# Linear attention and channel mix on one core: first two batches transposed on TensorE, v loads on the software queue, engine orders planned anew

## The chip, the cores and the metric

The kernel runs on one core of a Trainium2 chip (trn2). The metric is the device time of one execution in microseconds (us). TensorE is called PE here, VectorE DVE, ScalarE ACT, GpSimd POOL and SyncE SP, as in the profile.

## What is computed

Eight batches, eight heads, 576 positions, head width 64, 128 features. The attention output of a batch, [576, 512], is the input of a channel mix with hidden width 1024.

```python
def phi(x):
    proj = np.einsum('bhsd,df->bhsf', x, w_phi)
    proj = proj - np.max(np.abs(proj), axis=-1, keepdims=True)
    return np.concatenate([np.exp(proj), np.exp(-proj)], axis=-1)
q_p, k_p = (phi(q), phi(k))
kv = np.einsum('bhsf,bhsd->bhfd', k_p, v)
z = np.sum(k_p, axis=2)
num = np.einsum('bhsf,bhfd->bhsd', q_p, kv)
den = np.einsum('bhsf,bhf->bhs', q_p, z)[..., None] + 1e-06
# num / den, as x [B, S, 512], goes into:
xk = mu_k * x + (1.0 - mu_k) * x_prev
xr = mu_r * x + (1.0 - mu_r) * x_prev
k = np.maximum(xk @ w_k, 0.0)
v = k * k @ w_v
r = 1.0 / (1.0 + np.exp(-(xr @ w_r)))
return (r * v).astype(np.float32)
```

## The kernel before

The unit of the attention part is a pair of heads; there are 32 pairs, four to a batch. A position is split as 64 rows times 9 columns, so that two heads fill the 128 partitions and a pair's k or q is a [128, 576] tile. The steps of a pair have short names in the code, which the texts use. PE projects q and k (`qp`, `kp`, L418); DVE takes the largest absolute value of each row and column group, negated (`rq` L435, `rk` L430); POOL writes it as two bf16 parts (`mh`, L454 and L455); PE transposes that (`mt`, L459), DVE copies it out of PSUM (`mc`, L463), and PE adds it to the projections of k and q (`ka` L468, `qt` L476 and L482). ACT takes the exponentials, two for k (`ea`, `eb`, L445) and two for q (`qa`, `qb`, L489). POOL copies v into a tile with a column of ones (`vc`, L439), PE forms kv (`kv`, L504 and L510), ACT evicts it (`kc`, L515), PE forms numerator and denominator (`nd`, L523 and L528), DVE divides (`rd`, L535 and L537), PE transposes the result (`xt`, L545), and DVE writes it to `xs` (`xe`, L551 to L556), takes the difference of neighbours (`df`, L560) and mixes (`xa`, `xb`, L566). The ninth column of k and of q is done for several pairs at once, in steps whose names end in `e` (`tp`, `rt`, `mhe` L342 and L343, `mte`, and so on).

When all four pairs of a batch are mixed, its channel mix follows in 512-column pieces: eight `h` (four matmuls each, L636), ACT's relu (`rl`, L643), POOL's square (`sq`, L650), four `r` with a tanh, and four `v` (eight matmuls each, L671), which DVE scales into `ob` (L678) and SP stores (L685). The last 128 columns of two batches are done together (L712 to L788).

Loads: for each batch POOL's software queue loads k and q (`lk`, `lq`, L256, f32 in HBM and bf16 in `nat`), SP transposes both with one DMA (`tr`, L265) into `qkT`, and SP loads v in f32 (`lv`, L261). Batch 0 is loaded in three parts: pair 0, pair 1, and pairs 2 and 3. There are two buffers each of `nat`, `qkT` and `vt`: the load of k of batch b can start when the transpose of batch b - 2 has read `nat`. The three weights are loaded on POOL's queue (L291).

The order of the work is not written out by hand. Each step is entered with `op(name, engine, width, due, fn, deps, alloc, rel)`, and `Plan.order` (L45) simulates the engines with these widths and the delays `LAG` and `SWITCH`: for each engine it looks at up to twelve steps whose dependences are done, takes those that can start within 0.12 of the earliest, and of these the one with the least `due`. The instructions of an engine are then emitted in that order, and each engine works through its own strictly in order. Due times come from a spacing of T = 8.2 per pair.

```python
op(f"lk{tag}", "POOL", 0.7, due, ld(0), alloc=al("nat"), chain="lk")
op(f"tr{tag}", "SP", 0.6, due, tr, [f"lk{tag}.d", f"lq{tag}.d"], alloc=al("qkT"),
   rel=[("nat", b)])
```

In the simulation `nat` counts as free when the SP step `tr` ends, and that is 0.6 wide; on the chip it is free when the transpose has landed.

Of the kernel before, what the change touches and what calls it, by code (L numbers as in the profile page):

```python
# [15 lines left out]
LAG = {"PE": 0.25, "ACT": 0.2, "DVE": 0.15, "POOL": 0.2, "SP": 0.05, "DMA": 1.8}  # L16


SWITCH = 0.12


class Plan:
# [4 lines left out]
    def __init__(self):  # L27
        self.ops = []
        self.by_name = {}
        self.last = {}  # L30

    def op(self, name, eng, w, due, fn, deps=(), alloc=(), rel=(), chain=None, mode=0):
# [6 lines left out]
        o = dict(name=name, eng=eng, w=w, due=due, fn=fn, deps=tuple(deps),  # L39
# [5 lines left out]
    def order(self, bufs, loose=()):  # L45
# [3 lines left out]
        self.mode = 0  # L49
        slots = {t: [None] * bufs[t] for t in loose}  # L50
# [15 lines left out]
        while len(out) < n:  # L66
            best = None
            for e, ql in queues.items():
# [44 lines left out]
            free[e] = t + o["w"]  # L113
            end[o["name"]] = free[e]
# [23 lines left out]
def kernel(  # L138
# [108 lines left out]
    def add_load(b, a0, a1, due, first):  # L247
# [20 lines left out]
        g = 1.0 * n  # L268
        op(f"lk{tag}", "POOL", 0.7, due, ld(0), alloc=al("nat"), chain="lk")
        op(f"lk{tag}.d", "DMA", g, due, None, [f"lk{tag}"])  # L270
        op(f"lq{tag}", "POOL", 0.7, due, ld(1), [f"lk{tag}"])
        op(f"lq{tag}.d", "DMA", g, due, None, [f"lq{tag}"])
        op(f"tr{tag}", "SP", 0.6, due, tr, [f"lk{tag}.d", f"lq{tag}.d"], alloc=al("qkT"),
           rel=[("nat", b)])
        op(f"tr{tag}.d", "DMA", 1.5 * n, due, None, [f"tr{tag}"])
        op(f"lv{tag}", "SP", 0.6, due + 0.1, ldv, alloc=al("vt"), chain="lv")
        op(f"lv{tag}.d", "DMA", g, due + 0.1, None, [f"lv{tag}"])

    parts = {b: [(0, NP)] for b in range(B)}
    parts[0] = [(0, 1), (1, 2), (2, 4)]  # L280
    for b in range(B):
        for i, (a0, a1) in enumerate(parts[b]):
            add_load(b, a0, a1, ((4 * b - 6) * T if b > 1 else -50 + 10 * b + i), i == 0)

    def part_of(b, a):
        for (a0, a1) in parts[b]:
            if a0 <= a < a1:
                return f"{b}.{a0}"
# [15 lines left out]
    op("wvs", "DVE", 1.2, 3.2 * T,  # L304
# [5 lines left out]
    def ptile(key, name):  # L310
        return psum.tile([128, 2, 512], FP, name=name, tag=f"P{plan.place[key]}")

    def motile(key, name):
        return psum.tile([128, 512], FP, name=name, tag=f"M{plan.place[key]}")

    def add_edge(b, a0, a1, first, due):
# [57 lines left out]
        def eqe():  # L374
# [29 lines left out]
    def add_pair(n):  # L404
# [3 lines left out]
        d0 = n * T  # L408
        pt = part_of(b, a)
# [163 lines left out]
        op("qp" + N, "PE", 0.25, d0, qp, [f"tr{pt}.d", "dve1"], alloc=[("P", ("P", "q" + N))], chain="qp",  # L573
# [257 lines left out]
```

## Time and profile before

| | |
|---|---|
| median of 2 runs | 414.72 us (414.13 to 415.3) |
| profiled execution | 413.09 us |
| its span, first to last instruction | 411.3 us |
| time around the span | 1.8 us |
| mean granted TensorE clock | 0.942 of full speed |
| HBM read, written | 33.62 MB, 9.44 MB |

The profile is one execution. The page gives each engine's busy time. The timeline lists instructions in order of time, with the idle time of the engine before them in brackets and what ended it. The view by windows gives busy time of each engine, granted clock and DMA share for stretches of 5 us. The waits list who waited for whom. DMA issues are listed with the time from issue to landing.

### The profile page before, as it was taken

The page shows a single profiled execution, that of the slowest core. Times are in us where ns is not written, and L with a number is a line of the kernel's source. Part 1 is how long each engine was busy: PE and PEld are TensorE (multiplying, and loading weights), DVE is VectorE, ACT ScalarE, POOL GpSimd, SP SyncE. Part 2 cuts the span into 40 slices and gives each one's busy share as a digit, 9 for nine tenths or more (in the row PEclk, how much of TensorE's full clock was granted, in tenths as well). Part 3 has the DMA queues.
Part 4 walks back from the last instruction along what each step waited for, and adds up shares of the span by engine and source line. Part 5 has one row for each costly group of instructions (what it writes and reads, how often), then busy time and mean ns, then how long its engine had stood idle before and what let it go on. Part 6 is the DMA issues. An engine that isn't in the chain of part 4 may idle for free. (4 is left out here: it accounts for less than half of the span.)

```text
span 411.3 us, 8965 instructions
## 1 busy us (share of the span) xinstructions
PE 307.0 (75%) x3712; PEld 169.8 (41%) x3758; DVE 254.1 (62%) x456; ACT 209.6 (51%) x309; POOL 137.5 (33%) x237
## 2 busy tenths in 40 slices
PE   0046347867859779977778679977896979979895
PEld 0025235532435445534425345534453534535352
DVE  2035437996749786694845886595859566666312
ACT  0035235725717846657327646659285555665340
POOL 6042241164341461553323163145013420341450
PEclk9999999596989999997969899999999689999999
DMA  8989999953595008921792007402720002202214
GB/s 203 241 138 240 176 201 227 129 92 115 108 178 165 2 2 153 226 97 27 134 241 50 2 2 142 105 0 39 129 55 0 2 15 56 62 0 45 61 26 102
DMA packets 59063, 41.01 MB, mean 100 GB/s; under 512 B 39952, under 2 KB 49808, under 8 KB 59024
## 3 DMA queue, kind: packets, MB, share of 16 engines
q1 hardware_dynamic: 48416, 28.39, 31.2%
q0 software_dynamic: 10608, 12.06, 18.6%
q8 instruction: 29, 0.48, 0.5%
q14 instruction: 10, 0.08, 0.1%
HBM read 33.62 MB, written 9.44 MB: 105 GB/s over the span
## 5 line engine op out<-in xcount | busy, mean ns | idle before, releaser
L650 POOL TENSOR_TENSOR kk<-krelu 128x512 bf16<-128x512 bf16 x64 | 67.1, 1062 | 98.9 <-ACT krelu L643 98.8
L445 ACT ACTIVATE k<-ps_k 128x1024 bf16<-128x1024 f32 x64 | 62.3, 1029 | 47.5 <-PE ps_k L468 33.5
L636 PE MATMUL ps_h<-xk,wk_bf 128*128 128x512 bf16 x233 | 66.9, 402 | 5.3 <-ACT krelu L643 1.7
L671 PE MATMUL ps_v<-wv_bf,kk 128*128 128x512 bf16 x245 | 62.7, 396 | 3.3 <-DVE ob L678 1.4
L489 ACT ACTIVATE q<-ps_qT 128x1024 bf16<-128x1024 f32 x64 | 62.3, 1036 | 5.3 <-PE ps_qT L482 5.2
L643 ACT ACTIVATE krelu<-ps_h 128x512 bf16<-128x512 f32 x64 | 38.3, 613 | 45.6 <-PE ps_h L636 40.0
L678 DVE SCALAR_TENSOR_TENSOR ob<-rt,ps_v 128x512 f32<-128x512 bf16 x32 | 22.0, 687 | 46.0 <-issue 21.0
L435 DVE TENSOR_REDUCE nm<-ps_q 128x8 f32<-128x1024 f32 x32 | 39.0, 1220 | 13.3 <-PE ps_q L418 13.2
L664 ACT ACTIVATE rt<-ps_r 128x512 bf16<-128x512 f32 x32 | 19.2, 601 | 50.7 <-PE ps_r L657 50.2
L430 DVE TENSOR_REDUCE nm<-ps_k 128x8 f32<-128x1024 f32 x32 | 39.0, 1218 | 4.6 <-PE ps_k L418 4.5
L657 PE MATMUL ps_r<-wr_bf,xr 128*128 128x512 bf16 x117 | 34.5, 401 | 5.1 <-ACT krelu L733 2.1
L671 PEld LDWEIGHTS <-kk 128*128 128x128 bf16 x256 | 24.1, 100 | 33.0 <-issue 8.2
L636 PEld LDWEIGHTS <-wk_bf 128*128 128x128 bf16 x256 | 22.8, 101 | 30.5 <-issue 9.3
L566 DVE SCALAR_TENSOR_TENSOR xr<-diff,mu_r_t,xs 128x576 bf16<-128x576 bf16 x32 | 33.5, 1046 | 0.0
L454 POOL CAST mhl<-nm 128x16 bf16<-128x16 f32 x32 | 6.8, 212 | 69.7 <-DVE nm L430 69.7
L566 DVE SCALAR_TENSOR_TENSOR xk<-diff,mu_k_t,xs 128x576 bf16<-128x576 bf16 x32 | 28.9, 903 | 1.1
L537 DVE TENSOR_TENSOR x_sc<-ps_nd,rden 128x640 bf16<-128x640 f32 x32 | 26.4, 824 | 1.1
L504 PE MATMUL ps_kv<-v,k 64*128 64x65 bf16 x1024 | 25.4, 202 | 2.0 <-ACT k L445 1.7
L504 PEld LDWEIGHTS <-k 64*128 64x128 bf16 x1024 | 22.6, 102 | 9.6 <-issue 6.8
L333 DVE TENSOR_REDUCE me<-ps_e 128x8 f32<-128x1024 f32 (+2 forms) x10 | 10.1, 1007 | 25.8 <-PE ps_e L327 25.8
L418 PEld LDWEIGHTS <-qkT 64*128 64x128 bf16 x512 | 18.5, 102 | 17.9 <-issue 14.4
L459 PE MATMUL ps_m<-ident,mhl 128*128 128x128 bf16 x32 | 7.6, 238 | 24.0 <-POOL mhl L455 21.7
(74 smaller groups left out, 451.2 us busy)
## 6 DMA issues: line engine op xcount, KB each, us to landing
out_dram<-ob SPq DMA_DIRECT2D x72, 128.0 KB, 2.4
vt<-in_v_dram SPq DMA_DIRECT2D x7, 1152.0 KB, 9.6
nat<-in_k_dram POOLq DMA_DIRECT2D x7, 576.0 KB, 6.7
nat<-in_q_dram POOLq DMA_DIRECT2D x7, 576.0 KB, 10.7
wk_bf<-in_moe_w_k_dram POOLq DMA_DIRECT2D x1, 1024.0 KB, 15.0
wv_bf<-in_moe_w_v_dram POOLq DMA_DIRECT2D x1, 1024.0 KB, 21.0
vt<-in_v_dram SPq DMA_DIRECT2D x2, 288.0 KB, 4.8
vt<-in_v_dram SPq DMA_DIRECT2D x1, 576.0 KB, 7.0
```

The source lines that it names most:

```text
L430: nc.vector.tensor_reduce(s["nm"][:, 0, :], s["k"].rearrange("p a (g f) -> p (a g) f", f=128), axis=AX.X, op=ALU.max, apply_absolute_value ...
L435: nc.vector.tensor_reduce(s["nm"][:, 1, :], s["q"].rearrange("p a (g f) -> p (a g) f", f=128), axis=AX.X, op=ALU.max, apply_absolute_value ...
L445: nc.scalar.activation(s[f"k{pn}"], s["k"].rearrange("p a (g f) -> p (a g) f", f=128), AF.Exp, scale=(1.0 if pn == 0 else -1.0))
L489: nc.scalar.activation(t.rearrange("f h (c p) -> f c h p", c=8), s["qT"].rearrange("f a (g h p) -> f (a g) h p", g=4, h=2), AF.Exp, scale= ...
L504: nc.tensor.matmul(ps[:, hh, pn * 65:(pn + 1) * 65], lhsT=s[f"k{pn}"][r, c, :], rhs=vb[r, a, 2 * g + par, :], start=(pn == 0 and c == 0), ...
L537: nc.vector.tensor_tensor(s["x"].rearrange("p (b s) d -> p b s d", b=2), ndv[:, :, :, 0:64], s["rd"].to_broadcast([128, 2, 5, 64]), op=ALU ...
L566: nc.vector.scalar_tensor_tensor(out=t[:, a, (b % 2) * S:(b % 2 + 1) * S], in0=s["d"], scalar=mu[:, a:a + 1], in1=xs[:, a, 0:S], op0=ALU.m ...
L636: nc.tensor.matmul(ps, lhsT=wk_bf[:, c, fc * 128:(fc + 1) * 128], rhs=xkt[bp][:, c, m0:m0 + 512], start=(c == 0), stop=(c == NDC - 1))
L643: nc.scalar.activation(s["kr", fc], s[fc], AF.Relu)
L650: nc.gpsimd.tensor_tensor(s["kk"][:, fc, :], s["kr", fc], s["kr", fc], op=ALU.mult)
L657: nc.tensor.matmul(ps, lhsT=xrt[bp][:, c, m0 + ci * 128:m0 + (ci + 1) * 128], rhs=wr_bf[:, c, :], start=(c == 0), stop=(c == NDC - 1))
L671: nc.tensor.matmul(ps, lhsT=s["kk"][:, fc, ci * 128:(ci + 1) * 128], rhs=wv_bf[:, fc, :], start=(fc == 0), stop=(fc == NFC - 1))
```

## The change

- **Batch 0, pair 0.** k is loaded in f32 by SP's hardware queue (`hk`) and q by ACT's (`hq`); DVE casts k into `nat` (`lk0.0.d`), ACT casts q (`lq0.0.d`).
- **Batches 0 and 1.** No DMA transpose. For each of the eight pairs PE transposes nine 128x128 blocks into one of the three double PSUM banks "P" (`pt`); DVE copies five of them to `qkT` (`pa`), ACT four (`pb`). Batch 1 is loaded in two parts.
- **v** of every batch is loaded on POOL's software queue, cast to bf16 on the way.
- **Order of POOL's queue.** `lk`, `lq`, `lv` of all batches stand in one chain: batches 0 and 1, the weights (before: behind the transpose of batch 1), then batches 2 to 7.
- **Plan.** Due times are now pair number times 8.90 plus an offset for each kind of step (table `OFF`). The widths and delays are new: `tr` is 5.7 on SP instead of 0.6, `xe` 0.97 instead of 0.75, `mc` 0.22 instead of 0.16, `df` 0.46 instead of 0.4. Steps marked `port` (POOL's `mh`, `vc`, `sq`; DVE's `df`, `xa`, `xb`) do not start in the simulation while the other engine runs one of them. The last batch has no due times of its own any more. `ob` has four buffers instead of three.

What the steps compute is otherwise unchanged.

```diff
-LAG = {"PE": 0.25, "ACT": 0.2, "DVE": 0.15, "POOL": 0.2, "SP": 0.05, "DMA": 1.8}
-
-
-SWITCH = 0.12
+LAG = {"PE": 0.2, "ACT": 0.12, "DVE": 0.1, "POOL": 0.15, "SP": 0.05, "DMA": 1.8, "NONE": 0.0}
+
+
+SWITCH = 0.1
+
+
+PACE = 8.90
+OFF = {
+    "qp": -0.6, "kp": 4.2, "rq": 11, "rk": -31.8, "mh": 16.9, "mt": -15.1, "mc": -54.9, "ka": -19.2,
...
+    "rt": 42.7, "mhe": -40.3, "mte": -13.2, "mce": -44.7, "kae": -2.7, "ekt": 105.3, "pt": -33.4,
...
+    "lv": -12.2, "h0": 18.8, "h1": -28.7, "h2": 42.5, "h3": 57.8, "r0": 39.7, "h4": 62, "h5": 35.3,
+    "h6": 16.3, "h7": 32.1, "r1": 70, "v0": 90.5, "r2": 72.6, "v1": 87.3, "r3": 63.4, "v2": 60.2,
...
+        due = at
+        if isinstance(at, tuple):
+            due = at[1] * self.T + sum(self.off[x] for x in (at[0],) + at[2:])
...
+                if e in ("DVE", "POOL"):
+                    other = port["POOL" if e == "DVE" else "DVE"]
+                    cands = [(max(t, other) if o["port"] else t, o) for (t, o) in cands]
...
         def ldv():
-            t = get(vt, b, inp, [128, NP, X], FP, "vt")
-            nc.sync.dma_start(out=t[:, a0:a1, :], in_=heads(v, b, a0, a1))
+            t = get(vt, b, inp, [128, NP, X], BF, "vt")
+            nc.gpsimd.dma_start(out=t[:, a0:a1, :], in_=heads(v, b, a0, a1))
+
+        def pt(b, a):
+            def f():
+
+                i = NP * b + a
+                ps = ptile(("P", f"pt{i}"), "ps_pt")
+                pb = ps.rearrange("p a x -> p (a x)").bitcast(BF).rearrange("p (a g t) -> p a g t", a=2, t=128)
+                st["pb", i] = pb
+                for g in range(R):
+                    bk, o = divmod(g, 5)
+                    nc.tensor.transpose(pb[:, bk, o, :], nat[b][:, a, g * 128:(g + 1) * 128], ident)
+            return f
+
+        def pc(b, a, bk):
+            def f():
+                t = get(qkT, b, inp, [128, NP * R, 128], BF, "qkT")
+                n_ = 5 - bk
+                o = t[:, R * a + 5 * bk:R * a + 5 * bk + n_, :]
+                src = st["pb", NP * b + a][:, bk, 0:n_, :]
+                if bk == 0:
+                    nc.vector.tensor_copy(o, src)
+                else:
+                    nc.scalar.copy(o, src)
+            return f
...
+        if b == 0 and a0 == 0:
+            def hk():
+                st["kq"] = inp.tile([128, 2, X], FP, name="kq0", bufs=1)
+                nc.sync.dma_start(out=st["kq"][:, 0, :], in_=heads(k, 0, 0, 1)[:, 0, :])
+
+            def hq():
+                nc.scalar.dma_start(out=st["kq"][:, 1, :], in_=heads(q, 0, 0, 1)[:, 0, :])
...
+        else:
+            op(f"lk{tag}", "POOL", 0.75, at("lk"), ld(0), ["ident"], alloc=al("nat"), chain="ld")
...
+            op(f"lq{tag}", "POOL", 0.75, at("lq"), ld(1), [f"lk{tag}"], chain="ld")
...
+        op(f"lv{tag}", "POOL", 0.75, at("lv"), ldv, ["ident"], alloc=al("vt"), chain="ld")
...
+            op(f"tr{tag}", "SP", 5.7, at("tr"), tr, [f"lk{tag}.d", f"lq{tag}.d"], alloc=al("qkT"),
+               rel=[("nat", b)])
...
+    NPT = 2
+    lparts = {b: [(0, NP)] for b in range(B)}
+    lparts[0] = [(0, 1), (1, 2), (2, 4)]
+    lparts[1] = [(0, 2), (2, 4)]
...
+            for i, (a0, a1) in enumerate(lparts[b]):
+                add_load(b, a0, a1, (lambda kd, b=b, i=i: (kd, 4 * b) if b > 1 else -90 + 10 * b + i),
+                         i == 0)
...
+        op(nm_, "POOL", 0.75, i - 8, ldw(dst, src), [f"lv1.2"], chain="ld")
```

## Rows read from the trace of the kernel before

**Rows 1.** The page, part 1: busy time, share of the span, instructions.

```profile
PE 307.0 (75%) x3712; PEld 169.8 (41%) x3758; DVE 254.1 (62%) x456; ACT 209.6 (51%) x309; POOL 137.5 (33%) x237
```

**Rows 2.** Timeline, first 28 us: start, duration, engine, line, operation, count [idle before].

```profile
1.24 0.73 POOL L256 DMA_DIRECT2D nat<-in_k_dram  x1 [0.80 <-POOLq L815]
6.67 0.78 POOL L256 DMA_DIRECT2D nat<-in_q_dram  x1
6.70 19.20 SPq L265 DMA_TRANSPOSE qkT<-nat  x3
24.00 0.29 PE L327 MATMUL ps_e<-wph,qkT 64*128 64x128 bf16 x2 [24.00 <-DMA qkT<-nat]
24.82 0.19 POOL L342 CAST mhlt<-me 128x1 bf16<-128x1 f32 x1 [16.70 <-DVE me L333]
27.18 0.20 POOL L454 CAST mhl<-nm 128x16 bf16<-128x16 f32 x1 [0.89 <-DVE nm L430]
```

**Rows 3.** DMA issues of three stretches: 1 to 1.9, 6.6 to 7.4, 42.3 to 43 us.

```profile
nat<-in_k_dram POOLq DMA_DIRECT2D x1, 144.0 KB, 3.4
...
nat<-in_q_dram POOLq DMA_DIRECT2D x1, 576.0 KB, 16.2
...
wv_bf<-in_moe_w_v_dram POOLq DMA_DIRECT2D x1, 1024.0 KB, 21.0
```

**Rows 4.** Timeline, 40 to 56 us.

```profile
42.35 0.91 POOL L291 DMA_DIRECT2D wv_bf<-in_moe_w_v_dram  x1
...
44.07 1.22 DVE L430 TENSOR_REDUCE nm<-ps_k 128x8 f32<-128x1024 f32 x1
...
54.22 0.76 POOL L256 DMA_DIRECT2D nat<-in_k_dram  x1 [10.96 <-DMA qkT<-nat]
...
55.54 0.29 PE L459 MATMUL ps_m<-ident,mhl 128*128 128x128 bf16 x1 [9.51 <-POOL mhl L455]
```

**Rows 5.** Waits: engine, line, waited for: us in total, times, longest.

```profile
POOL nat L256 <- DMA qkT<-nat: 43.7, 5, 11.0
```

**Rows 6.** Timeline, around 115 and around 202 us.

```profile
114.62 0.80 POOL L256 DMA_DIRECT2D nat<-in_k_dram  x1 [8.26 <-DMA qkT<-nat]
...
202.49 0.80 POOL L256 DMA_DIRECT2D nat<-in_k_dram  x1 [10.43 <-DMA qkT<-nat]
```

**Rows 7.** Windows of 5 us: length, busy us (instructions) by engine, clock, DMA, GB/s.

```profile
90.00:95.00 5.00, 1.03 (x4) 0.38 (x5) 4.92 (x8) 0.92 (x2) 3.88 (x6) 0.92 0.00 0
...
115.00:120.00 5.00, 1.46 (x11) 0.73 (x12) 1.20 (x3) 0.00 (x0) 4.00 (x8) 0.81 0.90 147
...
205.00:210.00 5.00, 1.78 (x4) 0.69 (x6) 4.50 (x6) 0.34 (x1) 3.09 (x5) 0.68 1.20 203
210.00:215.00 5.00, 4.69 (x23) 1.64 (x23) 1.13 (x2) 0.99 (x2) 0.42 (x2) 0.63 0.86 308
...
360.00:365.00 5.00, 3.16 (x30) 1.29 (x28) 4.89 (x10) 1.42 (x3) 3.02 (x5) 1.00 0.00 0
```

**Rows 8.** Groups by line and shape: count | busy us, mean ns | idle before.

```profile
L566 DVE SCALAR_TENSOR_TENSOR xr<-diff,mu_r_t,xs 128x576 bf16<-128x576 bf16 x32 | 33.5, 1046 | 0.0
L566 DVE SCALAR_TENSOR_TENSOR xk<-diff,mu_k_t,xs 128x576 bf16<-128x576 bf16 x32 | 28.9, 903 | 1.1
L545 PE MATMUL ps_x<-ident,x_sc 128*128 128x128 bf16 x160 | 15.9, 236 | 5.9 <-DVE mT L463 4.7 <-DVE x_sc L537 0.5
L551 DVE COPY xs<-ps_x 128x512 bf16<-128x512 bf16 x32 | 13.5, 420 | 16.7 <-PE ps_x L545 16.7
```

**Rows 9.** Timeline, 77 to 80 us.

```profile
77.15 0.81 DVE L566 SCALAR_TENSOR_TENSOR xk<-diff,mu_k_t,xs 128x576 bf16<-128x576 bf16 x1
...
78.78 0.78 POOL L256 DMA_DIRECT2D nat<-in_k_dram  x1 [4.98 <-DMA qkT<-nat]
```

**Rows 10.** The chain that ended last, in order of time: start, us, what.

```profile
385.28 1.89 PE ps_h L636 x8
...
406.78 0.69 DVE ob L762
```

More of the change, by code (lines that the diff above doesn't have):

```diff
@@ L30, in __init__, with op @@
         self.last = {}
-    def op(self, name, eng, w, due, fn, deps=(), alloc=(), rel=(), chain=None, mode=0):
+    def op(self, name, eng, w, at, fn, deps=(), alloc=(), rel=(), chain=None, mode=0, port=False):
+        due = at
+        if isinstance(at, tuple):
+            due = at[1] * self.T + sum(self.off[x] for x in (at[0],) + at[2:])
         deps = list(deps)
@@ L49, in order @@
         self.mode = 0
+        port = {"DVE": 0.0, "POOL": 0.0}
         slots = {t: [None] * bufs[t] for t in loose}
@@ L113, in order @@
             free[e] = t + o["w"]
+            if o["port"]:
+                port[e] = free[e]
             end[o["name"]] = free[e]
@@ L233, with ptile, motile @@
     op("dve3", "DVE", 0.8, -7, c_dve3, ["ident"])
+    st = {}
+    def ptile(key, name):
+        return psum.tile([128, 2, 512], FP, name=name, tag=f"P{plan.place[key]}")
+    def motile(key, name):
+        return psum.tile([128, 512], FP, name=name, tag=f"M{plan.place[key]}")
     nat, qkT, vt = {}, {}, {}
@@ L275, in add_load @@
[L275 to L285, printed above, removed]
+        g = 0.95 * n
@@ new lines, in add_load @@
+        op(f"lv{tag}", "POOL", 0.75, at("lv"), ldv, ["ident"], alloc=al("vt"), chain="ld")
+        op(f"lv{tag}.d", "DMA", g, at("lv"), None, [f"lv{tag}"])
+        if b < NPT:
+            for a in range(a0, a1):
+                i = NP * b + a
+                op(f"pt{i}", "PE", 0.55, ("pt", i), pt(b, a), [f"lk{tag}.d", f"lq{tag}.d", "dve3"],
+                   alloc=[("P", ("P", f"pt{i}"))] + (al("qkT") if a == a0 else []), rel=[("nat", b)],
+                   chain="pt")
+                op(f"pa{i}", "DVE", 0.42, ("pa", i), pc(b, a, 0), [f"pt{i}"], rel=[("P", f"pt{i}")])
+                op(f"pb{i}", "ACT", 0.6, ("pb", i), pc(b, a, 1), [f"pt{i}"], rel=[("P", f"pt{i}")])
+                op(f"tr{i}", "NONE", 0, 0, None, [f"pa{i}", f"pb{i}"])
+        else:
+            op(f"tr{tag}", "SP", 5.7, at("tr"), tr, [f"lk{tag}.d", f"lq{tag}.d"], alloc=al("qkT"),
+               rel=[("nat", b)])
+            op(f"tr{tag}.d", "DMA", 4, at("tr"), None, [f"tr{tag}"])
+            for a in range(a0, a1):
+                op(f"tr{NP * b + a}", "NONE", 0, 0, None, [f"tr{tag}.d"])
@@ L303, with add_edge @@
     op("mus.d", "DMA", 0.3, -3, None, ["mus"])
-    op("wvs", "DVE", 1.2, 3.2 * T,
+    op("wvs", "DVE", 1.2, 20,
        lambda: nc.vector.tensor_scalar(wv_bf, wv_bf, 0.5, None, op0=ALU.mult), ["wv.d"])
     tkp, tkn, tqp, tqn = {}, {}, {}, {}
[L310 to L316, printed above, removed]
+    def add_edge(b, a0, a1, first, it):
         tag = f"{b}.{a0}"
@@ L611 @@
+        op("df" + N, "DVE", 0.46, ("df", n), df, ["xe" + N], port=True, alloc=al("d"), chain="df")
+        op("xa" + N, "DVE", 0.75, ("xa", n), mix(0), ["df" + N, "mus.d"], port=True)
+        op("xb" + N, "DVE", 0.75, ("xb", n), mix(1), ["xa" + N], port=True, rel=[("xs", b), ("d", n)])
     for n in range(B * NP):
```

181 lines of the change are left out of this document (92 added, 89 removed), and 5 rows, old and new, of the table OFF.

## Prediction

> **What bounds the kernel now.** I read the page first: PE is the busiest engine, and still idle for 411.3 - 307.0 = 104.3 us of the span [rows 1]. So no engine is full over the whole span, and the question is in which stretches something else sets the pace. The timeline gives the first: PE's first matmul starts at 24.00 us, and the row names the transposing DMA as what it waited for; that DMA's instruction for batch 0 stood on SP from 6.70 for 19.20 us [rows 2]. The second stretch follows at 46 us. The last reduction of pair 2, of which POOL needs the result, began at 44.07 and took 1.22 us, but POOL had gone on in its order to the load of k that waits for the transpose of batch 1, and stood there for 10.96 us; PE was idle for 9.51 us before the `mt` behind it [rows 4]. The waits show that this is a pattern: POOL stood 43.7 us in five such loads [rows 5], two of them at 114.62 and 202.49 [rows 6]. The windows then show two kinds of stretches with little PE work later on [rows 7]. Just behind those two loads PE has 1.46 and 1.78 us in 5 us. And there are seven windows of 5 us (the first at 90, the last at 360) in which DVE is busy 4.88 to 4.93 us and PE at most 3.21; PE's idle time in the seven adds up to 16.1 us. The chain of waits shows only the end, where PE runs the last channel mix back to back from 385.28 on [rows 10].
>
> **The change, part by part.**
>
> *Start (A).* The transpose of batch 0 goes, so the 24.00 is no longer what sets the start. What sets it next? POOL. Its order now has, by due time, `ident`, then thirteen loads (due -90 to -79), then `mhe` of pair 0 (due 1.4 x 8.9 - 40.3 = -28), the three weights (due -8 to -6) and `mh` of pair 0 (due 17). POOL's first load began at 1.24 and a load takes 0.73 to 0.80 us of POOL [rows 2, 6]. With 0.5 us for `ident` and 13 x 0.75 = 9.8, `mhe` starts at 11.5; it is four instructions of 0.19 us [rows 2], with the gaps some 1.0; three weights at 0.75 to 0.91 [rows 2, 4] are 2.4; `mh` of pair 0 then stands at 14.9 instead of 27.18 [rows 2]. That is -12.3. The data is there by then: the first load of 144 KB on the software queue landed in 3.4 us [rows 3], so f32 k and q should land by 5, casts and nine PE transposes follow (a PE transpose lasts 236 ns, the copy of a 512-column tile out of PSUM 420 ns [rows 8]), and PE's first projection comes at some 7 to 8 us. If POOL's queue were no gate, the gain would be 24.0 - 7 = 17; if the queue fills up, there is none (third rival). I take 12.3.
>
> *The stall at 46 us (B).* With the transposes of batches 0 and 1 on PE, `nat` of both is free as soon as PE has read it, and the loads of batches 2 and 3 wait for no DMA. The 9.51 us of PE idleness [rows 4] go; what is late next is DVE's work for pairs 2 and 3, which runs without a gap of that size elsewhere. I take -9, with 0 as the other end, should the weights or loads hold POOL at that place instead.
>
> *Later loads (C).* Batches 4 to 7 still wait for a transposing DMA. The plan now takes `tr` as 5.7 us instead of 0.6, and the transposes from then on need a little more than that, so loads will be put later into POOL's order and the waits of 5 to 10 us shrink. How much of those reached PE: behind the load at 114.62 PE idled 5 - 1.46 = 3.5, behind the one at 202.49 5 - 1.78 = 3.2, and the next window ran at a granted clock of 0.63, which costs 0.37 x 4.69 = 1.7 [rows 6, 7]. Together 8.4. I take -6, ends 0 and -8.4.
>
> *DVE and POOL (D).* The mixing steps take 1046 and 903 ns on average [rows 8] where an undisturbed one takes 0.81 [rows 9]: 32 x (0.24 + 0.09) = 10.6 us of DVE time lost in overlap with POOL's work. The plan now keeps these steps apart, and its DVE widths are those of the trace (`xe` was 0.22 too short per pair, 7 us in all). If that dissolves the seven stretches in which DVE holds PE up, 16.1 us come back [rows 7]; if a new order only moves them, nothing. I take half, -8, the middle between the two, since the rows show the overlap but not what another order makes of it.
>
> *Added work (E).* Nine transposes in each of eight pairs at the spacing of L545 (15.9 us for 160 [rows 8], 0.1 each) are 7 us of PE, 8 x 0.42 = 3.4 us of DVE, and by the plan's width of 0.6 some 5 us of ACT. They fall into the first 60 us, where PE, DVE and ACT have idle time; pair 0's are in (A) already. If the cover were gone, the longest of them would cost 7. I take +2.
>
> v on the software queue puts seven more loads of 0.8 us each on POOL after the start; POOL is busy for 33% [rows 1], so I cost them at nothing; if each delayed an `mh`, it would be 6 us. SP has a shorter queue: its transposes and stores no longer stand behind v loads that wait for POOL.
>
> Sum against the profiled execution: 413.1 - 12.3 - 9 - 6 - 8 + 2 = 379.8. The median shown is 1.6 above that execution, so I put 381.
>
> **One rule against the change.** Loads issued by POOL beside DVE work took as long as without it: 0.78 us at 78.78 amid mixing steps [rows 9], 0.78 us at 6.67 [rows 2]. The Trainium skill, page "SBUF — State Buffer", section "SBUF: two separate sides", says the opposite can happen: descriptors of such loads are written by GpSimd, and while VectorE runs an operation in a two-port mode they cannot be written; it gives 3.1 us instead of 0.62 for one load. By that figure the sixteen first loads would add 16 x 2.3 = 37 us to the start; by the rows they add nothing. No row here shows such a load slowed by DVE, and this is the page that stands beside the third rival.
>
> **The rivals.**
>
> 1. *Only the start and the stall.* The new order of steady state is no better: C and D are 0. For it speaks that the old order, too, was planned, and still left 104.3 us of PE idle [rows 1]. Against it: the two causes that the rows name are now in the plan. 413.1 - 12.3 - 9 + 2 + 1.6 = 395. Without B it is 404.
>
> 2. *The order fits the chip much better.* Of the 104.3 us idle [rows 1], 24.0 and 9.5 are A and B; 70.8 remain. If half of these go in place of C and D: 413.1 - 12.3 - 9 - 35 + 2 + 1.6 = 360; if 45 go, 350.
>
> 3. *POOL is held by its own loads (the other side).* Sixteen loads are issued in one go, and every `mh` stands behind them. Before, at most eight stood so. If POOL can issue only as room comes free, the time is that of the transfers: the loads of batches 0 and 1 ran from 1.24 to 6.67 + 16.2 = 22.9, the weights from 40.9 (two issues of 0.75 before 42.35) to 42.35 + 21.0 = 63.4 [rows 2 to 4], so 21.6 + 22.5 = 44 us, and `mh` of pair 0 would come at 45, 18 later than before: 413.1 + 18 - 9 + 2 + 1.6 = 426. It decides from the point where that `mh` is later than 42.5: then A is +15.3 and the sum 423, 2% above. Against it: the eight issues up to 6.67 show no growth, 0.73 us for the first and 0.78 for the last, with most of their data still to land [rows 2, 3].
>
> 4. *A loose end.* The last batch loses its own due times. Before, PE ran its pieces back to back from 385.28 to the last `ob` at 406.78 [rows 10]. If the pieces now wait for one another, the tail grows, at most by about that chain's 21 us: with 1 it gives 395 + 20 = 415, no measurable change; from 11 us of loss it eats what makes the change faster.
>
> **How the numbers follow.** Forecast 0.56 (its own range 367 to 394), first rival 0.18, second 0.15, third 0.04, fourth 0.07. The range goes from 350 (second rival's far end) to 404 (first rival without B); it leaves out the third and fourth, and the parts of the second that go further. About 2% is what a measurement of this kernel can tell from no change: 406.4 to 423.0. Forecast, first and second rival lie below it, 0.89 together, of which I take off 0.02 for sums of small losses: faster 0.87. The fourth gives no change, with these losses 0.08; slower is the third with a little more, 0.05.
>
> **What would show it.** (A) PE's first matmuls are transposes at about 5 us, the first projection at 7 to 8, and `mh` of pair 0 at about 15, directly behind three weight loads; a first `mh` beyond 25 makes A wrong. (B) No idle stretch of PE over 5 us between 15 and 60, and no POOL wait for `qkT` there. (C) POOL's waits for the DMA transpose below 15 us in total instead of 43.7. (D) Mixing steps near 0.85 us on average, and fewer than four 5 us windows with DVE above 4.85 and PE below 3.3. (E) The copies out of the new transposes at 0.4 (DVE) and 0.6 us (ACT). The prediction is wrong if the mixing steps stay at 0.9 to 1.05 and the dips of PE remain as many (then 395), or if PE's idle time falls by far more than 35 us (then 360 or less).

## The result, and the profile after

The changed kernel takes 332.43 us (median of 2 runs, 332.42 to 332.44) against 414.72. The ratio is 0.8016 with a 95% interval of 0.7967 to 0.8065: 82.3 us less, where 33.7 were forecast. The direction was right; the time lies 17.6 us below the low end of the range.

The page of after: busy time of each engine, PE by 40 slices, the granted clock, and the chain that ended last (answers to [rows 1]).

```profile
span 330.6 us, 9088 instructions
PE 293.4 (89%) x3784; PEld 170.6 (52%) x3830; DVE 247.8 (75%) x465; ACT 215.7 (65%) x318; POOL 148.4 (45%) x248
...
PE   1687777698999999999999999999989999999994
...
PEclk9997756799999999999999999999999999999998
...
PE 65%; DVE 20%; ACT 5%; POOL 4%; issue 3%; DMA 1%; SPq 0%; DVEq 0%; ACTq 0%; POOLq 0%
```

PE's idle time fell from 104.3 to 330.6 - 293.4 = 37.2 us, and its busy time from 307.0 to 293.4: 67.1 + 13.6 = 80.7, the whole difference of the spans (411.3 - 330.6). From the eleventh slice on PE is full, at nearly full clock. The chain now follows PE through 65% of the span. In the trace of before it was 5%, the last channel mix alone [rows 10].

Where the 67.1 came from is seen by stages. The view by windows, of before first, then of after: length, busy time of PE, PEld, DVE, ACT and POOL with instruction counts, granted clock, DMA share, GB/s.

```profile
0.00:25.00 25.00, 1.00 (x18) 0.88 (x18) 2.88 (x17) 0.16 (x1) 7.19 (x16) 1.00 1.07 221
25.00:65.00 40.00, 22.35 (x308) 14.80 (x305) 18.55 (x35) 18.05 (x31) 14.20 (x38) 1.00 1.09 192
65.00:385.00 320.00, 262.46 (x3275) 143.86 (x3318) 228.99 (x401) 182.82 (x265) 105.93 (x174) 0.93 0.40 82
385.00:411.30 26.30, 21.17 (x118) 10.23 (x119) 3.67 (x6) 8.56 (x15) 10.18 (x10) 1.00 0.28 60
```

```profile
0.00:25.00 25.00, 13.78 (x158) 9.86 (x160) 11.83 (x31) 10.06 (x17) 19.48 (x39) 1.00 1.08 189
25.00:65.00 40.00, 28.84 (x466) 21.08 (x462) 32.17 (x60) 24.54 (x38) 13.85 (x32) 0.67 1.00 169
65.00:325.00 260.00, 250.01 (x3167) 139.57 (x3212) 203.06 (x373) 181.12 (x264) 115.10 (x178) 1.00 0.46 86
325.00:330.60 5.60, 0.74 (x4) 0.13 (x2) 0.69 (x1) 0.00 (x0) 0.00 (x0) 0.83 0.44 94
```

In the first 65 us PE's idle time went from 65 - 23.35 = 41.7 to 65 - 42.62 = 22.4 us, 19.3 less; the forecast had 21.3 there (A and B). Behind 65 us it went from 62.7 to 14.9, 47.8 less; the forecast had 14 (C and D). The prediction was right about the start and far too low about the rest. In the long stage the granted clock rose from 0.93 to 1.00 of 2.4 GHz. Ahead of it, between 25 and 65 us, it fell from 1.00 to 0.67: PE is busy for longer there than before, but much of that at 1.2 GHz. What the start still costs is in this stage.

The start, in the timeline of after (start, duration, engine, line, instruction; in brackets the idle time before it and what ended it; answers to [rows 2]):

```profile
4.65 0.46 DVE L339 CAST nat<-kq 128x576 bf16<-128x576 f32 x1 [2.00 <-DMA kq<-in_k_dram]
5.17 0.88 PEld L305 LDWEIGHTS <-nat 128*128 128x128 bf16 x9 [5.17 <-DVE nat L339]
6.75 0.48 DVE L315 COPY qkT<-ps_pt 128x640 bf16<-128x640 bf16 x1
7.91 0.61 PE L517 MATMUL ps_q<-wph,qkT 64*128 64x128 bf16 x8 [1.60 <-ACT qkT L317]
10.79 0.70 POOL L294 DMA_DIRECT2D vt<-in_v_dram  x1 [0.81 <-DMA nat<-in_k_dram]
15.08 0.89 POOL L395 DMA_DIRECT2D wv_bf<-in_moe_w_v_dram  x1 [0.66 <-DMA nat<-in_k_dram]
15.96 0.21 POOL L553 CAST mhl<-nm 128x16 bf16<-128x16 f32 x1
...
164.46 0.82 POOL L289 DMA_DIRECT2D nat<-in_k_dram  x1 [4.83 <-DMA qkT<-nat]
```

PE transposes from 5.17 us on and projects from 7.91 on; `mh` of pair 0 stands at 15.96 behind three weight loads. The last line is the longest of the four waits for a transposing DMA that are left. The waits of POOL in after (total, times, longest; answers to [rows 5]):

```profile
POOL nat L289 <- DMA qkT<-nat: 14.4, 4, 4.8
POOL nat L289 <- PE ps_pt L305: 3.4, 1, 3.4
```

Four of the windows of 5 us in after (two answer to [rows 7]):

```profile
50.00:55.00 5.00, 4.37 (x89) 3.38 (x85) 4.76 (x11) 3.65 (x6) 0.00 (x0) 0.50 0.44 67
55.00:60.00 5.00, 3.10 (x52) 2.06 (x51) 4.90 (x10) 2.17 (x3) 2.77 (x5) 0.94 1.18 202
90.00:95.00 5.00, 4.84 (x82) 2.90 (x82) 3.90 (x11) 3.39 (x5) 2.30 (x3) 1.00 0.98 171
205.00:210.00 5.00, 4.95 (x56) 2.70 (x56) 4.34 (x10) 4.20 (x6) 1.97 (x4) 1.00 0.02 3
```

Before, 22 full windows had PE below 3.3 us, with 69.4 us of its idle time; after there are 9, with 24.0: eight in the first 65 us and one at the very end. The window at 55 is the only one left in which DVE is full and PE is not. Outside these dips the idle time fell too, from some 35 to 13.

The groups by line in after (mean duration in ns is the last number before the second bar; the first two answer to [rows 8], the others are the new steps):

```profile
L665 DVE SCALAR_TENSOR_TENSOR xr<-diff,mu_r_t,xs 128x576 bf16<-128x576 bf16 x32 | 28.4, 891 | 0.0
L665 DVE SCALAR_TENSOR_TENSOR xk<-diff,mu_k_t,xs 128x576 bf16<-128x576 bf16 x32 | 27.7, 867 | 0.9
...
L305 PE MATMUL ps_pt<-ident,nat 128*128 128x128 bf16 x72 | 8.9, 310 | 6.9 <-DVE nat L339 5.2 <-ACT qkT L317 0.9 <-ACT k L544 0.5
L317 ACT COPY qkT<-ps_pt 128x512 bf16<-128x512 bf16 x8 | 4.7, 587 | 12.4 <-DVE qkT L315 9.2 <-PE ps_pt L305 3.1
L315 DVE COPY qkT<-ps_pt 128x640 bf16<-128x640 bf16 x8 | 3.8, 488 | 5.9 <-PE ps_pt L305 5.3 <-ACT qkT L317 0.6
```

### The profile page after: what moved, and what is told of

Its sections match the earlier page's. It is cut to its first block, busy times and chain, and to the rows that moved or that the text cites. A ratio compares the mean times of both kernels' runs of the same rounds, so it can differ in the third digit from the quotient of the medians.

```text
span 330.6 us, 9088 instructions
## 1 busy us (share of the span) xinstructions
PE 293.4 (89%) x3784; PEld 170.6 (52%) x3830; DVE 247.8 (75%) x465; ACT 215.7 (65%) x318; POOL 148.4 (45%) x248
## 3 DMA queue, kind: packets, MB, share of 16 engines
q0 software_dynamic: 14624, 16.48, 30.3%
## 4 chain that ended last, share of the span: by engine, by line
PE 65%; DVE 20%; ACT 5%; POOL 4%; issue 3%; DMA 1%; SPq 0%; DVEq 0%; ACTq 0%; POOLq 0%
PE ps_v L760 16%; PE ps_h L725 12%; PE ps_r L746 5%; DVE nm L534 5%; PE ps_kv L603 5%; PE ps_nd L622 4%; DVE nm L529 4%; PE ps_x L644 3%; DVE x_sc L636 3%; PE ps_k L567 3%; PE ps_q L517 2%; PE ps_ve L845 2%; ACT q L588 2%; PE ps_pt L305 2%; POOL kk L739 2%
## 5 line engine op out<-in xcount | busy, mean ns | idle before, releaser
L544 ACT ACTIVATE k<-ps_k 128x1024 bf16<-128x1024 f32 x64 | 64.3, 1033 | 13.1 <-PE ps_k L567 12.4
L725 PE MATMUL ps_h<-xk,wk_bf 128*128 128x512 bf16 x237 | 62.2, 383 | 2.1 <-ACT krelu L732 0.7
L760 PE MATMUL ps_v<-wv_bf,kk 128*128 128x512 bf16 x243 | 58.5, 380 | 1.2 <-issue 0.6
L767 DVE SCALAR_TENSOR_TENSOR ob<-rt,ps_v 128x512 f32<-128x512 bf16 x32 | 21.9, 684 | 29.1 <-PE ps_v L760 28.2
L553 POOL CAST mhl<-nm 128x16 bf16<-128x16 f32 x32 | 10.0, 312 | 51.5 <-DVE nm L529 51.5
L746 PE MATMUL ps_r<-wr_bf,xr 128*128 128x512 bf16 x114 | 30.8, 380 | 1.5 <-issue 0.6
L665 DVE SCALAR_TENSOR_TENSOR xr<-diff,mu_r_t,xs 128x576 bf16<-128x576 bf16 x32 | 28.4, 891 | 0.0
L665 DVE SCALAR_TENSOR_TENSOR xk<-diff,mu_k_t,xs 128x576 bf16<-128x576 bf16 x32 | 27.7, 867 | 0.9
L614 ACT CAST kv<-ps_kv 128x260 bf16<-128x260 f32 x32 | 12.1, 379 | 22.4 <-PE ps_kv L609 22.1
L622 PEld LDWEIGHTS <-q 128*128 128x128 bf16 x512 | 20.5, 99 | 10.5 <-issue 3.6
L622 PE MATMUL ps_nd<-kv,q 128*128 128x65 bf16 x512 | 21.9, 195 | 4.1 <-ACT q L588 4.0
## 6 DMA issues: line engine op xcount, KB each, us to landing
nat<-in_q_dram POOLq DMA_DIRECT2D x6, 576.0 KB, 11.1
```

The lines of the kernel that those rows point to most:

```text
L544: nc.scalar.activation(s[f"k{pn}"], s["k"].rearrange("p a (g f) -> p (a g) f", f=128), AF.Exp, scale=(1.0 if pn == 0 else -1.0))
L622: nc.tensor.matmul(ps[:, bk, o * 65:(o + 1) * 65], lhsT=s[f"q{pn}"][:, h, G * 128:(G + 1) * 128], rhs=s["kv"][:, h, pn, :], start=(o == 0 ...
L665: nc.vector.scalar_tensor_tensor(out=t[:, a, (b % 2) * S:(b % 2 + 1) * S], in0=s["d"], scalar=mu[:, a:a + 1], in1=xs[:, a, 0:S], op0=ALU.m ...
L725: nc.tensor.matmul(ps, lhsT=wk_bf[:, c, fc * 128:(fc + 1) * 128], rhs=xkt[bp][:, c, m0:m0 + 512], start=(c == 0), stop=(c == NDC - 1))
L746: nc.tensor.matmul(ps, lhsT=xrt[bp][:, c, m0 + ci * 128:m0 + (ci + 1) * 128], rhs=wr_bf[:, c, :], start=(c == 0), stop=(c == NDC - 1))
L760: nc.tensor.matmul(ps, lhsT=s["kk"][:, fc, ci * 128:(ci + 1) * 128], rhs=wv_bf[:, fc, :], start=(fc == 0), stop=(fc == NFC - 1))
```

## The experiments

All kernels compute the same as before and after; only loads, buffers, or the planner's numbers differ. Three things limit the reading. A change of a width, delay or due time makes the planner order the whole kernel anew, so such a run prices that number within the plan, not one wait by itself; the four runs with a buffer or a load moved (three buffers, early loads) keep the order otherwise. All runs but one are single times; the kernel before took 409.95 to 417.18 us in all its runs, so I read nothing from differences under 5 us. And the trace of after lacks 46 matmuls (3784 against 3830 in the run with early loads; that of before lacks as many), which stand in it as idle time: where a difference to after is split into idle and busy time, some 3 us may belong to the other side. "+" is against after, 332.4.

### New loads with the old plan, and the new plan with the old loads

```diff
-LAG = {"PE": 0.2, "ACT": 0.12, "DVE": 0.1, "POOL": 0.15, "SP": 0.05, "DMA": 1.8, "NONE": 0.0}
+LAG = {"PE": 0.25, "ACT": 0.2, "DVE": 0.15, "POOL": 0.2, "SP": 0.05, "DMA": 1.8, "NONE": 0.0}
-            due = at[1] * self.T + sum(self.off[x] for x in (at[0],) + at[2:])
+            due = self.old_due(at)
-                    cands = [(max(t, other) if o["port"] else t, o) for (t, o) in cands]
+                    cands = list(cands)
-            op(f"tr{tag}", "SP", 5.7, at("tr"), tr, [f"lk{tag}.d", f"lq{tag}.d"], alloc=al("qkT"),
+            op(f"tr{tag}", "SP", 0.6, at("tr"), tr, [f"lk{tag}.d", f"lq{tag}.d"], alloc=al("qkT"),
```

(and the old widths of the other steps)

> New loads and transposes, but the plan's due times, widths, delays and port rule of the kernel before. Theory 'order' (the new order of the engines brought most of the 82 us, the new start some 20): about 394, between 385 and 403. Rival 'start' (PE transposes and the chained loads also free the later stretches, the order only follows): below 360.

Measured: 393.31 us, before 414.08. This is the time of the prediction's first rival, 395: start and stall alone are worth 20.8, and A + B + E came to 19.3. Three later waits for the transpose remain, 33.0 us in all, the one at 46 us is gone. Some 61 us of the change are in the plan.

```diff
-    NPT = 2
+    NPT = 0
-        if b == 0 and a0 == 0:
+        if False:
-            nc.gpsimd.dma_start(out=t[:, a0:a1, :], in_=heads(v, b, a0, a1))
+            nc.sync.dma_start(out=t[:, a0:a1, :], in_=heads(v, b, a0, a1))
```

(and the old order of the loads, with the weights behind the transpose of batch 1)

> The reverse: loads, DMA transposes and v loads as in the kernel before, with the new due times, widths, delays and port rule. Theory 'order': 345 to 358, the new start being worth some 13 to 25. Rival 'start': above 385.

Measured: 352.4 us (+20.0). PE's first projection again waits 24.3 us for the transposing DMA. So the two halves are nearly additive: about 20 for the loads, 61 for the plan.

### The plan's due times against its costs

```diff
-            due = at[1] * self.T + sum(self.off[x] for x in (at[0],) + at[2:])
+            due = self.old_due(at)
```

> The new kernel with the old due times alone (spacing 8.2, old offsets); new widths, delays and port rule stay. If within the order it is the due times that bring it: 380 to 395, close to the kernel with the whole old plan. Rival 'costs' (the better widths and the port rule bring it): below 355.

Measured: 373.28 (+40.9). POOL's waits for the transpose are 12.1 us, less than after's, so they are not what costs the 41.

The next run keeps the new due times and takes back widths, delays, the port rule and the width of `tr`.

```diff
-SWITCH = 0.1
+SWITCH = 0.12
-            op(f"tr{tag}", "SP", 5.7, at("tr"), tr, [f"lk{tag}.d", f"lq{tag}.d"], alloc=al("qkT"),
+            op(f"tr{tag}", "SP", 0.6, at("tr"), tr, [f"lk{tag}.d", f"lq{tag}.d"], alloc=al("qkT"),
-                    cands = [(max(t, other) if o["port"] else t, o) for (t, o) in cands]
+                    cands = list(cands)
```

> The new kernel with the old widths, delays, no port rule and the transpose 0.6 wide; new due times stay. If the due times bring it: 338 to 352. Rival 'costs': above 370.

Measured: 370.7 (+38.3), with 36.8 us of POOL's waits. From the 393.3 with both old, new costs alone bring 20.0, new due times alone 22.6, both together 60.9: 18 us come only from the two together. Neither is "the" cause.

### Single costs of the plan taken back

```diff
-            op(f"tr{tag}", "SP", 5.7, at("tr"), tr, [f"lk{tag}.d", f"lq{tag}.d"], alloc=al("qkT"),
+            op(f"tr{tag}", "SP", 0.6, at("tr"), tr, [f"lk{tag}.d", f"lq{tag}.d"], alloc=al("qkT"),
-            op(f"tr{tag}.d", "DMA", 4, at("tr"), None, [f"tr{tag}"])
+            op(f"tr{tag}.d", "DMA", 1.5 * n, at("tr"), None, [f"tr{tag}"])
```

> The new kernel with one width back: the DMA transpose 0.6 wide on SP and 1.5 per pair behind it, so the plan again believes the load buffer free at once. Old costs together gave 370.7 (e4), 38 more than the new kernel; this asks how much of that is POOL standing in front of loads. By step C of the prediction: 336 to 341, POOL's waits for the transposing DMA back above 25 us in total. Rival 'no part of it': 331 to 334.

Measured: 362.69 (+30.3). One number of the planner is worth nearly the whole forecast, five times the 6 of step C. Its waits:

```profile
POOL nat L289 <- DMA qkT<-nat: 36.0, 4, 13.8
```

```diff
-                    cands = [(max(t, other) if o["port"] else t, o) for (t, o) in cands]
+                    cands = list(cands)
```

> The new kernel without the port rule in the plan. By step D of the prediction, overlap of the mixing steps with POOL's work: 340 to 350, mixing steps back to 0.95 us and more on average. Rival 'the delays do it': 332 to 337.

Measured: 349.05 (+16.6). But the mixing steps take 927 (`xk`) and 847 ns (`xr`) against 867 and 891, no longer on average; the rule is worth its 17 us in the plan, and not by shorter mixing steps.

```diff
-        op("xe" + N, "DVE", 0.97, ("xe", n), xe, ["xt" + N], rel=[("mo", "x" + N)])
-        op("df" + N, "DVE", 0.46, ("df", n), df, ["xe" + N], port=True, alloc=al("d"), chain="df")
+        op("xe" + N, "DVE", 0.75, ("xe", n), xe, ["xt" + N], rel=[("mo", "x" + N)])
+        op("df" + N, "DVE", 0.4, ("df", n), df, ["xe" + N], port=True, alloc=al("d"), chain="df")
```

(and `qp`, `kp`, `mc`, `vc`, `qt`, `nd` at their old widths)

> The new kernel with the old widths of the pair's steps (xe 0.75, mc 0.16, df 0.4, qp, kp 0.25, qt 0.5, nd 0.7, vc 1.0). If the plan needs true DVE widths (xe alone is 7 us over 32 pairs): 338 to 348. Rival 'the delays do it': 332 to 337.

Measured: 344.03 (+11.6), mixing steps 955 and 890 ns.

```diff
-LAG = {"PE": 0.2, "ACT": 0.12, "DVE": 0.1, "POOL": 0.15, "SP": 0.05, "DMA": 1.8, "NONE": 0.0}
-SWITCH = 0.1
+LAG = {"PE": 0.25, "ACT": 0.2, "DVE": 0.15, "POOL": 0.2, "SP": 0.05, "DMA": 1.8, "NONE": 0.0}
+SWITCH = 0.12
```

> The new kernel with the old delays between engines and the old price of a PE mode switch. If port rule and widths carry the 38 us: 332 to 338. Rival 'the delays do it' (each hand-over is planned 0.05 to 0.08 us too late, so the order leaves room that the chip does not need and the due offsets no longer fit): 345 to 370.

Measured: 344.87 (+12.4). The delays count as much as the widths, and the prediction did not price them. The four single returns add up to 70.9, all four at once cost 38.3: they are not terms of a sum.

### The two tables of due times

```diff
-            due = at[1] * self.T + sum(self.off[x] for x in (at[0],) + at[2:])
+            due = self.old_due(at) if len(at) == 3 else at[1] * self.T + sum(self.off[x] for x in (at[0],) + at[2:])
```

Here the channel mix (entries with three parts) has the old due times, at the new spacing of 8.9; the next kernel has it the other way round, `len(at) == 2`: old for pairs and loads, new for the mix.

> The new kernel with the old due times for the steps of the channel mix alone (at the new spacing of 8.9 per pair: a batch's pieces due within 36 us instead of about 70); the pairs keep the new ones. All old due times cost 41 us (e3). If spreading the mix is the gain: 355 to 372. Rival 'the pair steps': 333 to 345.

> The other half: old due times for the steps of the pairs, the loads and the ninth column (at 8.9 per pair), new ones for the channel mix. If spreading the mix is the gain: 335 to 350. Rival 'the pair steps': 355 to 372. If both cost much, the two tables only work together.

Measured: 369.67 (+37.2) and 370.39 (+38.0). Either table alone loses nearly what both lose together (+40.9). The two losses differ in kind: with the old mix times 22.0 us are PE's busy time (315.4 instead of 293.4) and 15.3 its idle time; with the old pair times 13.6 and 24.4.

With the old mix times PE has five stretches of 9.0 to 13.7 us with no piece of the mix, where after has none over 3.4 and before none over 7.7. Within each of the five the granted clock falls to 0.50; its mean is 0.895 instead of 0.956. Two windows of the longest stretch, 171.0 to 184.7:

```profile
175.00:180.00 5.00, 3.04 (x43) 1.95 (x43) 4.54 (x8) 3.67 (x5) 0.57 (x2) 0.80 1.25 186
180.00:185.00 5.00, 4.06 (x75) 3.04 (x73) 4.47 (x10) 2.55 (x4) 3.06 (x5) 0.50 0.51 76
```

The steps of the pairs alone keep PE busy for 10.3 of these 13.7 us, and from 178.0 to 188.2 it runs at 1.2 GHz. That fits a mix used as filling between the steps of the pairs. Why the old pair times cost as much, and which entries of the tables do it, stays open.

### The wait itself: loads moved, order kept

```diff
+    for b in range(4, B):
+        i = next(j for j, o in enumerate(seq) if o["name"] == f"lk{b}.0")
+        o = seq.pop(i)
+        i = next(j for j, p in enumerate(seq) if p["name"] == f"tr{b - 2}.0")
+        seq.insert(i + 1, o)
```

> The new kernel with its order kept on every engine, save that on POOL the load of k of batches 4 to 7 stands directly behind the transpose that frees its buffer is issued, two to six POOL instructions earlier. The narrow transpose width (e5) cost 30 us, but it also changed the whole order. If POOL's standing in front of loads is what costs: waits for the transposing DMA at 30 us and more (14.4 in the new kernel), and the time 345 to 352. Rival 'the rest of the order did it': 331 to 338.

Measured: 361.12 (+28.7). Only four loads stand earlier in POOL's order, where they wait for the transpose. The waits, the windows and the timeline of this kernel:

```profile
POOL nat L289 <- DMA qkT<-nat: 36.5, 4, 13.8
```

```profile
90.00:95.00 5.00, 4.73 (x55) 2.75 (x55) 4.85 (x10) 4.45 (x6) 0.83 (x2) 1.00 0.74 136
95.00:100.00 5.00, 1.25 (x6) 0.39 (x4) 1.04 (x2) 0.00 (x0) 1.46 (x3) 0.96 0.81 155
100.00:105.00 5.00, 4.48 (x46) 2.21 (x47) 1.78 (x4) 2.31 (x3) 1.86 (x5) 0.50 1.10 164
```

```profile
98.54 0.81 POOL L289 DMA_DIRECT2D nat<-in_k_dram  x1 [7.71 <-DMA qkT<-nat]
99.96 0.20 POOL L553 CAST mhl<-nm 128x16 bf16<-128x16 f32 x1
100.52 0.29 PE L558 MATMUL ps_m<-ident,mhl 128*128 128x128 bf16 x1 [4.27 <-POOL mhl L554]
```

22.1 us more of waiting cost 28.7, of which 17.3 are PE's idle time (37.2 to 54.5) and 11.4 its busy time (293.4 to 304.8). PE is busy for 40.4 us at a granted clock of 0.50 here and for 23.2 in after; at half speed that is 8.6 of the 11.4. The lines show how: POOL stands for 7.71 us, the `mh` behind the load comes at 99.96, and only then PE's `mt`. By then not PE alone has run dry: DVE is busy for 1.04 and ACT for 0.00 us of the window at 95. In the next window PE is busy again, but at 0.50 of full clock, the 1.2 GHz level, with DVE at 1.78: the steps of the pairs fill up again one behind the other.

```diff
-                t = get(nat, b, inp, [128, NP, 2 * X], BF, "nat")
+                t = get(nat, b, inp, [128, NP, 2 * X], BF, "nat", bufs=3)
```

This is after with a third `nat`, the order unchanged: the remaining waits of 14.4 and 3.4 us go.

> The new kernel, its order unchanged on every engine, with a third buffer of nat, so that POOL's loads need not wait for the transpose of two batches before (17.8 us of such waits are left in the new kernel). If each us that POOL stands costs 1.3 us, as the early loads did (22 us more of waiting, 29 us more of time): 310 to 322, a version faster than both. Rival 'the waits that are left are covered, since PE is busy for over 4.7 of 5 us around them': 329 to 333.

Measured: 334.72 us (333.8 to 334.83, 4 runs), ratio to before 0.8091 (0.802 to 0.8161). The waits are gone and nothing is gained: where the plan puts these loads, POOL's wait is covered.

Early loads and a third buffer together (both edits above):

> The early loads (361.1) again, with the third buffer of nat: the same early place in POOL's order, but nothing to wait for there. If standing is the cost: back to 330 to 337, POOL's waits for the transposing DMA below 5 us. Rival 'the early place itself, or the load's traffic, costs': above 350.

Measured: 345.07. With the waits gone 16 of the 28.7 us come back, so at least that much of the run with early loads is the wait. 12.6 remain. The run with the third buffer alone has the same buffers and no such wait either, and is 10.4 us faster, so the early place itself costs. What the trace shows of it is that the loads now run beside the transposing DMA. The issues of the stretch 160 to 163 us (median us to landing), then a window and a line of the timeline behind them:

```profile
nat<-in_k_dram POOLq DMA_DIRECT2D x1, 576.0 KB, 9.9
qkT<-nat SPq DMA_TRANSPOSE x1, 26.0
```

```profile
175.00:180.00 5.00, 0.00 (x0) 0.00 (x0) 0.07 (x1) 0.00 (x0) 1.04 (x1) 0.87 1.48 147
```

```profile
181.34 0.61 PE L517 MATMUL ps_q<-wph,qkT 64*128 64x128 bf16 x8 [7.08 <-issue]
```

The transpose that lands in 7.3 us in after takes 26.0 here. PE stands for 7.08 us before the line at 181.34, but not for this landing, which comes at 186.90: the projection in that line is that of pair 19, whose batch was transposed by 138.42. The wait has no releaser in the profile ("issue"). SP stood in the transpose's instruction from 160.91 to 180.71, and the queue that carries instructions (q8, one packet of 16 KB every 7 to 12 us in this stretch of after) moved no packet between 156.1 and 178.9; PE may have stood for its own instructions behind the crowded transfers, but no run shows that.

### The same two edits in the kernel before

```diff
-        op(f"tr{tag}", "SP", 0.6, due, tr, [f"lk{tag}.d", f"lq{tag}.d"], alloc=al("qkT"),
+        op(f"tr{tag}", "SP", 5.7, due, tr, [f"lk{tag}.d", f"lq{tag}.d"], alloc=al("qkT"),
-        op(f"tr{tag}.d", "DMA", 1.5 * n, due, None, [f"tr{tag}"])
+        op(f"tr{tag}.d", "DMA", 4, due, None, [f"tr{tag}"])
```

> The kernel before with one number changed: the width of the DMA transpose in the plan, 5.7 on SP and 4 behind it, as in the new kernel. If that number alone carries what e5 lost: 380 to 395, and POOL's waits for the transpose below 25 us instead of 43.7. Rival 'it carries only in the new order': 405 to 420.

Measured: 391.26 us, before 410.4 (-19.1); POOL's waits fall from 43.7 to 11.1. Then before with a third `nat` buffer and its own order:

```diff
-                t = get(nat, b, inp, [128, NP, 2 * X], BF, "nat")
+                t = get(nat, b, inp, [128, NP, 2 * X], BF, "nat", bufs=3)
```

> The kernel before, its order unchanged, with a third buffer of nat: the 43.7 us that POOL stood in front of loads go without any new order. The prediction costed them at 9 + 6 = 15 us. If it was right on this: 396 to 402. If the size of that step was wrong, as the early loads suggest: 370 to 393. Rival 'nothing comes of it in the old order': above 408.

Measured: 396.56 us, before 415.48 (-18.9). So in the old order the waits cost about 19 net; B and C together were put at 15, with 17.4 as far end. Here too transposes land late beside loads, in 11.3 to 28.6 us for batches 2 to 5, so the waits alone may have cost more.

### Single loads taken back

```diff
-    NPT = 2
+    NPT = 0
```

> The new kernel with batches 0 and 1 transposed by DMA again; hardware loads of pair 0, v on the software queue and the chained loads stay. The old loads as a whole cost 20 us (e2). If PE's transposes are the part that counts: 346 to 353. Rival 'the first pair's hardware loads and the chain count': 333 to 340.

Measured: 365.57 (+33.1), more than the 20 of the run with all the old loads. Batches 0 and 1 are transposed by DMA again, now while all first loads stand in the queue: transposes land in up to 28.6 us, and PE waits 37.5 us for three. At 35 us nothing runs but DMA:

```profile
35.00:40.00 5.00, 0.00 (x0) 0.00 (x0) 0.00 (x0) 0.00 (x0) 0.00 (x0) 1.00 1.29 158
```

```diff
-            nc.gpsimd.dma_start(out=t[:, a0:a1, :], in_=heads(v, b, a0, a1))
+            nc.sync.dma_start(out=t[:, a0:a1, :], in_=heads(v, b, a0, a1))
-        op(f"lv{tag}", "POOL", 0.75, at("lv"), ldv, ["ident"], alloc=al("vt"), chain="ld")
+        op(f"lv{tag}", "SP", 0.6, at("lv"), ldv, alloc=al("vt"), chain="lv")
```

> The new kernel with the loads of v on SP's hardware queue in f32, as before, instead of in POOL's chain; the plan orders the engines anew with that. The prediction costed this edit at nothing. If it is worth nothing: 330 to 336. If the chain is worth something because loads beside a transposing DMA slow it (a transpose beside a load landed after 26.0 us in e14, 7.3 in the new kernel): 338 to 352, with transposes that land after 10 us and more.

Measured: 342.11 (+9.7). The transposes whose landing the trace has took 7.3 to 9.1 us, so it shows no delay of them by v in f32 on SP's queue; POOL's waits are 19.1. What the rest is, the new order or the queue, was not separated.

```diff
-        if b == 0 and a0 == 0:
+        if False:
```

> The new kernel with k and q of pair 0 on POOL's software queue, as before, at the head of its chain. By the prediction POOL sets the start, and two more loads of 0.75 us stand before the first mh: 333 to 337. Rival 'the early hardware loads are what makes the start': 340 and more, with PE's first transpose beyond 7 us instead of 5.2.

Measured: 344.37 (+11.9). Pair 0 on the software queue: PE's first transpose stands at 4.86 us, no later than the 5.17 of after. The hardware queues do not buy an earlier first transpose. The first `mh` stands at 17.86 instead of 15.96, near the 1.5 us of two more loads, and PE is idle for 14.6 instead of 11.2 us of the first 25. POOL waits 7.8 instead of 3.4 us for PE's transposes. The granted clock is 0.50 for 30.8 us between 43 and 78, but after has 27.3 such us between 28 and 66, so the slow clock hardly explains the loss. The cause of the rest was not settled.

## Why the prediction was wrong in size

**The step that failed.** C and D, 14 us together, were all that the sum had for the new plan, and the runs measure the plan at 61 (393.31 with the old plan, 332.43 with the new). The steps one by one:

**Start (A): right.** The projection came at 7.91 for "7 to 8" and `mh` of pair 0 at 15.96 for 14.9, from 27.18 [rows 2].

**The stall (B): right.** POOL's first wait for `qkT` is one of 2.62 us that ends at 61.94, and the run with the old plan has A, B and E together: 20.8 for 19.3. But by stages that run's first 65 us have only 13.4 us less idle time of PE (41.7 to 28.2); the total agrees better than the place.

**Later loads (C): mechanism right, size right for the old order only.** The waits are 14.4 us, "below 15". In the old order B and C measure 19 for 15. In the new order the same kind of wait cost 29 to 30. The prediction read its price from PE's idle time in one window behind two of the loads [rows 7], and took one slow window with it. The early loads show the rest: the engines behind PE run dry too, and PE's next stretch runs at half clock. That a dense order has no idle time left to take this up, and the old one had, fits these numbers but was not tested by itself.

**DVE and POOL (D): the step that failed most.** It took half of seven dips, 8 us. After has one dip of that kind, inside the first 65 us, so the 16.1 us there are gone; and the mixing steps did come down, to 867 and 891 ns from 903 and 1046, near 0.88 for the 0.85 said. But without the port rule they average 887 as well, so keeping them apart from POOL's steps is not what shortened them. And D's frame was too narrow. Behind 65 us the idle time fell by 47.8 us, and C and D gave 14. Of the 104.3 us idle, some 35 lay in windows with PE at 3.3 or more that the prediction never counted, and some 22 of these went. The delays (12.4), the widths (11.6), the port rule (16.6) and the due times (40.9) each cost that much when taken back alone; the prediction gave two of them one term and the other two none.

**Added work (E): right.** The copies take 488 and 587 ns for 0.4 and 0.6, the transposes 8.9 us of PE in all for 7.

**v at nothing: not shown.** Its run lost 9.7 us with an order of its own.

**The form of the sum.** It added gains of separate waits. The runs show that the plan's numbers act together (20.0 and 22.6 alone, 60.9 together). And the sum knew idle time alone: PE's busy time fell by 13.6 us although 8.9 us of transposes were added. The clock is a part of these 22.5: before, PE was busy for 40.8 us at 0.50, all behind 65 us; after, for 23.2 us, nearly all ahead of 65. At half speed the difference is 8.8 us; the other 13.7 were not traced to a cause. The only slow clock in the sum was the 1.7 us inside C.

**The rivals.** The second, an order that fits much better, is what happened; the prediction's own mark for it (idle time falling by far more than 35 us) was met with 67.1. Its far end of 45 of the 70.8 us was my choice, not read from a row, and set the low end of the range: 67.1 less the 19.3 of the first 65 us are 47.8, and 13.6 of busy time stood in no bound. The first is the time of the run with the old plan. The third shows itself faintly: in the first 16 us POOL stood a few times, for 0.26 to 0.81 us, before issuing a load until an earlier one had landed. The loads' own price held: 0.54 to 0.89 us for the 34 loads of after, and 0.81 at 127.64 while DVE copied `xs` at 127.96. The 3.1 us that the Trainium skill, page "SBUF — State Buffer", section "SBUF: two separate sides", gives for such a load under DVE's two-port modes is seen in no run here; the longest such instruction of any run took 1.31 us. Whether DVE's steps here run in such a mode, no trace tells. The fourth, a loose end, did not come.

## What to carry to other kernels

Where engines work through fixed orders, price a wait by everything that stands behind it on its engine, and by the slow clock that follows when the others run dry, not by one idle window; the same kind of wait was dearer in the dense order (22.1 us of it cost 28.7) than in the old one (43.7 us cost about 19). Give a planner the time at which a buffer is really free, the landing of the DMA that reads it: taking this one number back cost 30 us here, and with it a third buffer gained nothing more. In the old order the number alone and the third buffer alone each gained 19. When a whole order is planned anew, put an upper bound from all the idle time and all the slow clock behind the start, because the gains of single numbers do not add. And look where the slow clock goes: here it left the long stage and came up anew between 25 and 65 us.

## What was not expected of the hardware

- A transposing DMA that runs beside loads of the software queue landed in up to 27.1 us (early loads with a third buffer) and 28.6 (before with a third buffer; batches 0 and 1 by DMA) instead of 7.3 to 8.2 in after. Loads that a third buffer let start early gave 10.4 us of time back (345.07 against 334.72).
- After 4.27 us in which PE stood, the next window was granted 0.50 of the clock although PE was busy for 4.48 of its 5 us.
